# Reading x transposed from DRAM for ten token tiles, with a feature map and a weight sum moved between engines

## The chip, the cores and the metric

The kernel runs on one core of one Trainium2 chip. The metric is device time in microseconds (us) of one execution of the whole program. Engines are named as the profile names them: PE (TensorE matmul), PEld (its weight load), DVE (VectorE), ACT (ScalarE), POOL (GpSimd) and SP (SyncE, which here issues the DMAs).

## The reference

One block is computed over S = 2048 tokens of D = 576 features, in float32:

```
xn  = layernorm(x)                                # per token, eps 1e-5, no scale or shift
q, k, v = split(xn @ wqkv)                        # 32 heads of 18 features
phi(t) = where(t > 0, t + 1, exp(t)) + 1e-6
kv  = sum over tokens of phi(k)^T v               # per head, 18 x 18
z   = sum over tokens of phi(k)                   # per head
s   = ((phi(q) @ kv) / (phi(q) . z + 1e-6)) @ wo
g   = silu(gelu(xn @ w1 + b1) @ w2 + b2)          # hidden size F = 4608
out = x + s * g
```

## The kernel before, in words

Every matrix product is made of two-part operands: a tensor is rounded to a "hi" part (an ACT copy that casts to fp32r) and the remainder is its "lo" part (a DVE subtraction). A product then is hi*hi + hi*lo + lo*hi on PE. Two large products (w1 and w2) are cut into 2 x 2 blocks and done with seven block products instead of eight, so they need sums and differences of blocks (on POOL), whose hi and lo parts are formed as well.

The work has three phases, written one after the other. Within phases 1 and 2 every engine follows the program's order (`in_order()`), and in phase 3 DVE, ACT, POOL and PE do. So what an engine executes next is fixed by the code; an instruction that waits holds up all that is queued behind it on its engine.

**Phase 1** is a loop over 16 token tiles of 128 tokens (`for t in range(NT)`, L464). One turn is called a slot here. In slot t PE does: `project` into `pk` (k and the first part of v, 28 matmuls), `transpose_x(t + 1)` (five 128 x 128 transposes of the normalised x, L212), `state` of the tile before (its sum of phi(k)^T v into `ps_kva`, `ps_kvb`, L293), and `project` into `pv` (the rest of v, 14 matmuls). Around that, DVE takes the statistics of tile t + 2 (`layernorm`), ACT normalises it (`normalize_x`, L201), and ACT and DVE split the transposed x into `xh` and `xl`. The feature map `phi` is an ACT exponential (L262), a DVE minimum with 1 (L264), and a DVE maximum against the projection (L266). POOL adds phi(k) to `zacc` (L523), the source of z. PSUM has three two-bank buffers (`bank2`), handed out in turn to `pk`, `pt`, `pv`, and two one-bank buffers (`bank1`).

Beside this, phase 1 prepares weights for phase 3. For each of nine chunks of w2, `w2_sum` forms three block differences (`T_OPS = (5, 6, 4)`) on POOL, `w2_hi` and `w2_lo` split them on ACT and DVE, and `w2_store` writes them to DRAM; `we_sums`, `we_hi`, `we_lo` do the same for five groups of the last rows of w1. Four stores of x blocks to `x_dram` (`X_STORES`) are issued in slots 11 to 14, and `make_mask` runs on POOL in slot 7.

**Between phases 1 and 2** PE does `query(0)` (the q projection of tile 0), the last `state`, two matmuls into `zb_ps` that spread z over all partitions (L548), and `query(1)`. ACT copies `zb_ps` to `zb` (L549). Then ACT and DVE do `phi` for q of tiles 0 and 1 (`phi_query(0)`, `phi_query(1)`), and `fold_wo` multiplies the masked kv with wo: six blocks of two matmul results each (L604), written to `bank1` buffers in turn and copied out by ACT (L611, L613) or DVE (L609), before `query(2)`.

**Phase 2** is a loop over the tiles: `query(i)`, `transpose_p(i - 2)`, `attend(i - 4)` on PE, `phi_query(i)` and the denominators beside it.

**Phase 3** takes 18 steps, nine chunks of the hidden size for each half of the tokens. A step has 28 places (`NS = 28`). Places 0 to 13 are two `Up` units of seven block products each, in the order `UP = (1, 6, 7, 5, 2, 3, 4)`; places 14 to 27 are the `product` calls with w2, in the order `ORDER = (1, 2, 7, 4, 5, 3, 6)`. After each place, `at_step` emits what the plan put there: `base + place`. In the first half (steps 0 to 8) the plan also holds the preparation of w1 and w2: `sum7` on POOL at place 2, the `hi` and `lo` of w2 operands 1, 2 and 7 at places 3 to 6 (`PW2`), and loads of the operands 4, 5 and 6 that phase 1 stored. In the second half all operands are loaded. Within an `Up`, product 5 goes to the PSUM bank `E`, DVE adds it to `B` (L1047), and product 3, two products later, accumulates onto `E`, so it must wait for that addition. `HOps.S` forms the sums of the gelu outputs on POOL (L1111, L1114, L1117, L1120), and their `lo` parts are at L707, as are those of w2.

```
PW2 = {1: 3, 2: 4, 7: 5, 3: 20}
W2_SUMS_NEXT = {4: 21, 5: 23, 6: 27}
W2_SUMS_FIRST = {4: 4, 5: 6, 6: 10}
W2_LOADS = {0: (0, 1), 1: (2,), 3: (3,), 4: (4,), 6: (5,), 8: (6,), 9: (7,), 12: (8,)}
```

Of the kernel before, what the change touches and what calls it, by code (L numbers as in the profile page):

```python
# [15 lines left out]
P = 128  # L16
# [8 lines left out]
KT = 5  # L25
# [14 lines left out]


@with_exitstack
def linear_attention_gated_ffn(ctx, tc, x, wqkv, wo, w1, w1e, b1, w2, b2, out):
# [94 lines left out]
    ones = t1.tile([P, P], F32, name="ones", bufs=1)  # L138
    nc.gpsimd.memset(ones, 1.0)
# [4 lines left out]
    def make_mask():  # L144

        nc.gpsimd.memset(mf, 1.0)
# [26 lines left out]
    def layernorm(t):  # L173
# [3 lines left out]
        mv = t1.tile([P, 4], F32, tag="mv", name=f"mv{t}")  # L177
        nc.vector.bn_aggr(mv[:, 0:2], st)
        nc.vector.tensor_scalar_add(mv[:, 2:3], mv[:, 1:2], 1e-5)
        nc.gpsimd.tensor_tensor(mv[:, 3:4], mv[:, 2:3], nhalf, op=ALU.pow)  # L180
        stats[t] = mv
        if t == 0:
            xn[t] = t1.tile([P, 640], F32, tag="xn", name=f"xn{t}")
            for dst, src in norm_parts(t):
                nc.vector.tensor_scalar(dst, src, mv[:, 0:1], mv[:, 3:4], op0=SUB, op1=MUL)

    def offset(t):

        mv = stats[t]
        nc.vector.scalar_tensor_tensor(  # L190
            mv[:, 2:3], mv[:, 0:1], -1.0, mv[:, 3:4], op0=MUL, op1=MUL
        )
# [4 lines left out]
    def normalize_x(t):  # L197
        mv = stats.pop(t)
        xn[t] = t1.tile([P, 640], F32, tag="xn", name=f"xn{t}")
        for dst, src in norm_parts(t):  # L200
            nc.scalar.activation(dst, src, AF.Identity, scale=mv[:, 3:4], bias=mv[:, 2:3])  # L201
# [29 lines left out]

    PARTS = [p + str(k) for k in range(KT) for p in ("hh", "hl", "lh") if (p, k) != ("lh", KT - 1)]
# [25 lines left out]
    VB = 512 - HD  # L258

    def phi(pool, ps, name, between=lambda: None):  # L260
        e = pool.tile([P, D], F32, tag="e", name=f"e{name}")
        nc.scalar.activation(as2(e), ps[:, :, :HD], AF.Exp)  # L262
# [3 lines left out]
        nc.vector.scalar_tensor_tensor(  # L266
            as2(r), ps[:, :, :HD], 1.000001, as2(e), op0=ADD, op1=ALU.max
        )
        return r, e
# [17 lines left out]
    zacc = t1.tile([P, D], F32, name="zacc", bufs=1)  # L287
    ps_kv = []

    def state(t, k_t, v_t):  # L290
        for i, (g, n) in enumerate(GROUPS):
            dst = ps_kv[0][:n, g : g + n] if i < 4 else ps_kv[1][:n, :n]
            nc.tensor.matmul(  # L293
                dst, v_t[:, g : g + n], k_t[:, g : g + n],
                start=(t == 0 and i in (0, 4)), stop=(t == NT - 1), skip_group_check=True,
            )
# [3 lines left out]
    T_OPS = (5, 6, 4)  # L300
    w2raw, w2op = {}, {}

    def w2_load(c):
        if c == 2:
            t = x_hi(2, "w2r2")
        elif c == 5:
            t = x_hi(3, "w2r5")
        else:
            t = w2p.tile([P, CF * D], F32R, tag="w2r", name=f"w2r{c}")
        t = t.bitcast(F32) if c not in (2, 5) else t.bitcast(F32).rearrange("p a b -> p (a b)")  # L310
        nc.sync.dma_start(t[:, : CF * D], w2[c])
        w2raw[c] = t[:, : CF * D].rearrange("p (a r n d) -> p a r n d", a=2, r=2, n=2)

    def w2_block(c, i):

        B = lambda r, n: w2raw[c][:, :, r, n, :]
        return {
            5: (B(0, 0), B(0, 1), B(0, 0)),
            6: (B(1, 1), B(1, 1), B(0, 0)), 4: (B(1, 0), B(1, 0), B(1, 1)),
        }[i]  # L320

    def w2_sum(j):
        c, i = j // 3, T_OPS[j % 3]
        dst, a, b = w2_block(c, i)
        nc.gpsimd.tensor_tensor(dst, a, b, op=SUB)  # L325

    def w2_hi(j):
# [5 lines left out]
        nc.scalar.copy(w2op[j][:, 0], w2_block(j // 3, T_OPS[j % 3])[0])  # L333

    def w2_lo(j):
        c, i = j // 3, T_OPS[j % 3]
        t = w2op[j]
        nc.vector.tensor_tensor(t[:, 1], w2_block(c, i)[0], t[:, 0].bitcast(F32), op=SUB)

    def w2_store(j):  # L340
        c, i = j // 3, T_OPS[j % 3]
# [21 lines left out]
    def we_op(q, v):  # L363
        return we["h", q % 2][:, v * WB * P : (v + 1) * WB * P]
# [8 lines left out]
    def we_store(q):  # L373
        src = we["h", q % 2][:, : 2 * WB * P].bitcast(F32)
# [3 lines left out]
    W2_LOADS = {0: (0, 1), 1: (2,), 3: (3,), 4: (4,), 6: (5,), 8: (6,), 9: (7,), 12: (8,)}  # L378
    W2_SUMS = {}
    for j in range(3 * NC):  # L380
        W2_SUMS.setdefault(1 + j // 2, []).append(j)
# [52 lines left out]
    def query(t):  # L434
# [24 lines left out]
    X_STORES = {  # L459
        11: lambda: (0, xh[0][:, :4]), 12: lambda: (4, xl[0]),  # L460
        13: lambda: (10, xh[1][:, 2:4]), 14: lambda: (14, xl[1][:, 2:]),
    }
    raw_q = {}
    for t in range(NT):  # L464
        for n in (3, 4) if t == 0 else (t + 4,):
# [4 lines left out]
        if 0 < t < NT - 2:  # L470
            layernorm(t + 2)
        pk = bank2(f"pk{t}")
        v_t = t1.tile([P, D], F32, tag="v", name=f"v{t}")
        if t == 0:
# [8 lines left out]
            project(t, wv_h, wv_l, pv, FIRST_V[0], end=False)  # L483
        else:
            project(t, wkv_h, wkv_l, pk, cols=(slice(0, HD), slice(HD, D + VB)))
            k_t, _ = phi(t1, pk, f"k{t}", lambda: nc.scalar.copy(v_t[:, :VB], pk[:, 1, HD:]))
        if t + 1 < NT:
            if t + 1 in (8, 12):
                x_block((t + 1) // 4)
            transpose_x(t + 1)  # L490
        if t == 0:
            project(t, wv_h, wv_l, pv, FIRST_V[1], begin=False)
        for j in W2_SUMS.get(t - 1, ()):
            w2_hi(j)
        for j in W2_SUMS.get(t - 1, ()):
            w2_lo(j)
        if 2 <= t < 2 + WG:
            we_hi(t - 2), we_lo(t - 2)
        if t == 0:
            layernorm(2)  # L500
        if t + 2 < NT:
            offset(t + 2)
        if t == 0:
            k_t, _ = phi(t1, pk, f"k{t}")
# [4 lines left out]
        if t == 0:  # L509
            nc.scalar.copy(as2(v_t), pv[:, :, :HD])  # L510
        else:
            pv = bank2(f"pv{t}")
            project(t, wkv_h, wkv_l, pv, cols=(slice(D + VB, 2 * D),))
            nc.scalar.copy(v_t[:, VB:], pv[:, 0, : D - VB])
        if t + 2 < NT:
            normalize_x(t + 2)
        if t == 0:
            nc.gpsimd.memset(zacc, 0.0)
        for j in W2_SUMS.get(t, ()):
            w2_sum(j)  # L520
        if 1 <= t < 1 + WG:
            we_sums(t - 1)
        nc.gpsimd.tensor_tensor(zacc, zacc, k_t, op=ADD)  # L523
# [6 lines left out]
        if 2 <= t < 2 + WG:  # L530
            we_store(t - 2)
            if t < WG:
                we_load(t)
        for c in W2_LOADS.get(t, ()):
            w2_load(c)
        if t == KT + 2:
# [3 lines left out]
        if t in X_STORES:  # L540
            at, src = X_STORES[t]()
            nc.sync.dma_start(x_dram[:, at : at + src.shape[1]], src.bitcast(F32))
# [3 lines left out]
    zb_ps = bank2("zb_ps")  # L546
    for h in range(2):
        nc.tensor.matmul(zb_ps[:, h, :HD], ones, zacc[:, h * HD : (h + 1) * HD], start=True, stop=True)  # L548
    nc.scalar.copy(as2(zb), zb_ps[:, :, :HD])  # L549
# [3 lines left out]
    nc.vector.copy_predicated(kvz[:ln, D:], mask[:ln, 8:ln], ps_kv[1][:ln, 8:ln])  # L553
    ph1.close()
# [7 lines left out]
    def load_w2_raw(n):  # L562
        raw = w2rp.tile([P, CF // 2, 2, 2, HD], F32, tag="w2raw", name=f"w2raw{n}")
        nc.sync.dma_start(raw.rearrange("p a b n d -> p (a b n d)"), w2[n % NC])
# [392 lines left out]

    for i in range(1, NT + 4):
        if i < NT:
            query(i)  # L960
        if i == 1:
# [100 lines left out]
    class W2:  # L1062
# [5 lines left out]
        def load_raw(self):  # L1068
            self.raw = raw = load_w2_raw(self.n) if self.n else w2_raw0[0]
            self.B = lambda r, n: raw[:, :, r, n, :]  # L1070
# [4 lines left out]

        def plain(self, f):
            self.src["p", f] = self.raw[:, f // 2, f % 2]
# [301 lines left out]
    for step in range(n_chunks):  # L1379
# [139 lines left out]
```

## Time and profile before

| what | value |
| --- | --- |
| time, median of 3 runs | 1100.94 us (1100.39 to 1101.23) |
| the profiled execution's own time | 1101.18 us |
| its span, first to last instruction | 1099.5 us |
| PE busy | 1092.2 us (99%) |
| DVE busy | 809.3 us (74%) |
| ACT busy | 456.2 us (41%) |
| POOL busy | 452.0 us (41%) |
| granted TensorE clock | 1.000 |

The span lies inside the execution's own time. Busy time is the time in which an engine has an instruction under way. A timeline row gives the start, the time for all its instructions together, the engine, the source line, the operation, the tile written and those read, the shape, and in brackets how long the engine sat idle before and what ended that. A row of the chain that ended last gives the start, the time it holds, and its engine and line. Matmuls overlap at their ends, so a matmul row's time is a little more than its share of the chain.

### The profile page before, as it was taken

Reading aid. Unit: us, or ns where it says so; the run is one execution under the profiler, and the core shown is the slowest. Engines: PE = TensorE matmul, PEld = TensorE weight load, DVE = VectorE, ACT = ScalarE, POOL = GpSimd, SP = SyncE. Lnnn points to the kernel's source line nnn. Section 1 sums busy time; section 2 is a strip of 40 time slices with the busy share of each in tenths; the row PEclk is TensorE's granted clock in tenths of the full one; section 3 lists DMA queues with packets and bytes.
Section 4 is the critical chain, followed back from the end, with each engine's and each line's share of the span. In section 5 each row is a group of like instructions: output and inputs, shape, how many; then the busy total and the mean of one; then the engine's idle time right before and its main releaser. Section 6 shows DMA issues by size and latency. Waiting matters only on the chain.

```text
span 1099.5 us, 18157 instructions
## 1 busy us (share of the span) xinstructions
PE 1092.2 (99%) x6762; PEld 1006.8 (92%) x6762; DVE 809.3 (74%) x1162; ACT 456.2 (41%) x787; POOL 452.0 (41%) x392
## 2 busy tenths in 40 slices
PE   9999999999999999999999999999999999999998
PEld 8999989999998998989989899899898998989988
DVE  7786558989687887978878878667485574764866
ACT  5555444343644354454443544524234242242342
POOL 4786434333354452453534633324234143242340
PEclk9999999999999999999999999999999999999999
DMA  8697852575978659576595689978776676766452
GB/s 331 226 369 278 288 193 64 171 234 181 318 265 317 214 186 338 187 274 250 185 347 176 242 288 391 395 259 283 225 229 223 204 231 219 242 216 216 136 183 87
DMA packets 84655, 265.57 MB, mean 242 GB/s; under 512 B 9942, under 2 KB 20694, under 8 KB 80728
## 3 DMA queue, kind: packets, MB, share of 16 engines
q1 hardware_dynamic: 84568, 264.42, 68.7%
q8 instruction: 53, 0.87, 0.3%
q14 instruction: 34, 0.28, 0.1%
HBM read 166.69 MB, written 95.75 MB: 239 GB/s over the span
## 4 chain that ended last, share of the span: by engine, by line
PE 98%; DMA 0%; DVE 0%; issue 0%; ACT 0%; SPq 0%; DVEq 0%; ACTq 0%
PE pm L1154 35%; PE a L1021 10%; PE e L1021 10%; PE zy L1021 10%; PE pk L250 7%; PE ps_s L680 5%; PE pq L250 5%; PE b L1021 5%; PE pv L250 3%; PE pd L1270 2%; PE ps_kva L293 1%; PE ptp L662 1%; PE pt L212 1%; PE ps_kw L604 1%; DMA w<-wqkv 0%
## 5 line engine op out<-in xcount | busy, mean ns | idle before, releaser
L1160 DVE TENSOR_TENSOR macc<-pm,macc 128x576 f32<-128x576 f32 x218 | 163.6, 750 | 54.6 <-PE pm L1154 53.8
L704 ACT CAST h_h<-g 128x512 fp32r<-128x512 f32 x204 | 120.8, 620 | 132.5 <-PE pm L1154 131.4
L707 DVE TENSOR_TENSOR h_l<-g,h_h 128x512 fp32r<-128x512 f32 x204 | 164.9, 815 | 0.0
L1120 POOL TENSOR_TENSOR mid<-g 128x512 f32<-128x512 f32 x34 | 43.9, 1290 | 125.9 <-ACT g L1029 125.9
L1114 POOL TENSOR_TENSOR g<-g 128x512 f32<-128x512 f32 x34 | 54.8, 1613 | 56.9 <-DVE h_l L707 55.6
L1029 ACT ACTIVATE g<-b,b1c 128x512 f32<-128x512 f32 x36 | 24.8, 688 | 115.8 <-DVE b L1047 115.8
L1038 ACT COPY mid<-a 128x512 f32<-128x512 f32 x36 | 21.1, 587 | 117.2 <-PE a L1021 117.2
L750 POOL TENSOR_TENSOR w1raw<-w1raw 128x256 f32<-128x256 f32 x18 | 16.9, 939 | 122.0 <-DVE wa L766 122.0
L1041 DVE TENSOR_TENSOR mid<-b,mid 128x512 f32<-128x512 f32 x36 | 24.7, 686 | 44.6 <-PE b L1021 43.1
L1242 POOL TENSOR_TENSOR fin1l<-fin1h,fin1l 128x288 f32<-128x288 f32 x8 | 6.5, 810 | 121.6 <-DMA fin1l<-s_dram 107.2
L1117 POOL TENSOR_TENSOR g<-g 128x512 f32<-128x512 f32 x34 | 55.2, 1624 | 2.7
L1021 PE MATMUL a<-h0r,wa 128*128 128x512 f32 x144 | 50.4, 391 | 0.0
L1021 PE MATMUL a<-xh,wa 128*128 128x512 f32 x144 | 50.4, 390 | 0.0
L707 DVE TENSOR_TENSOR h_l<-mid,h_h 128x512 fp32r<-128x512 f32 x34 | 48.9, 1438 | 1.2
L1111 POOL TENSOR_TENSOR g<-g 128x512 f32<-128x512 f32 x34 | 46.8, 1376 | 2.7
L1047 DVE TENSOR_TENSOR b<-e,mid 128x512 f32<-128x512 f32 x36 | 25.2, 699 | 30.3 <-PE e L1021 30.3
L645 POOL TENSOR_TENSOR pbuf<-phiq,den 128x576 f32<-128x576 f32 x16 | 20.8, 1298 | 63.1 <-DVE den L644 44.3
L1044 DVE TENSOR_TENSOR mid<-zy,mid 128x512 f32<-128x512 f32 x36 | 24.9, 691 | 24.6 <-PE zy L1021 24.6
L325 POOL TENSOR_TENSOR w2r<-w2r 128x576 f32<-128x576 f32 x27 | 39.6, 1472 | 7.9 <-DMA w2r<-w 7.2
L250 PE MATMUL pk<-wkv_l,xh 128*128 128x288 f32 (+1 forms) x160 | 41.9, 343 | 0.1
L250 PE MATMUL pk<-wkv_h,xh 128*128 128x288 f32 (+1 forms) x160 | 41.3, 341 | 0.5 <-ACT wkv_h L280 0.5
L264 DVE TENSOR_SCALAR ek<-ek 128x576 f32<-128x576 f32 x16 | 12.8, 798 | 38.0 <-ACT ek L262 38.0
(826 smaller groups left out, 3563.7 us busy)
## 6 DMA issues: line engine op xcount, KB each, us to landing
we<-we_dram SPq DMA_DIRECT2D x36, 448.0 KB
op<-w2o SPq DMA_DIRECT2D x27, 576.0 KB
w2raw<-w SPq DMA_DIRECT2D x10, 1152.0 KB
w2r<-w SPq DMA_DIRECT2D x9, 1152.0 KB
w1raw<-w SPq DMA_DIRECT2D x18, 512.0 KB
op_a<-wa SPq DMA_DIRECT2D x18, 512.0 KB
op_c<-wc SPq DMA_DIRECT2D x18, 512.0 KB
op_d<-wd SPq DMA_DIRECT2D x18, 512.0 KB
```

The source lines that it names most:

```text
L250: nc.tensor.matmul(ps[:, h, : ws.stop - ws.start], st, w[:, k, ws], start=(begin and i == 0), stop=(end and i == len(seq) - 1), skip_group ...
L325: nc.gpsimd.tensor_tensor(dst, a, b, op=SUB)
L680: nc.tensor.matmul(ps[:, h, :HD], st[:, k, :], w[:, k, h * HD : (h + 1) * HD], start=(i == 0), stop=(i == len(seq) - 1),)
L704: nc.scalar.copy(pair[0], src)
L707: eng.tensor_tensor(pair[1], src, pair[0].bitcast(F32), op=SUB)
L1021: nc.tensor.matmul(ps, st, mv, start=first and n == 0, stop=n == len(seq) - 1, skip_group_check=True,)
L1111: tt(src[5, pr], A(1, 0), A(1, 1), op=ADD)
L1114: tt(src[6, pr], src[5, pr], A(0, 0), op=SUB)
L1117: tt(src[3, pr], A(0, 1), src[6, pr], op=SUB)
L1120: tt(src[7, pr], A(0, 0), A(1, 0), op=SUB)
L1154: nc.tensor.matmul(ps[:, q, :HD], hs[p][st][:, cs], m[:, p, :], start=(n == 0 and i not in CHAIN), stop=(n == 5), skip_group_check=True,)
L1160: nc.vector.tensor_tensor(dst, src, dst, op=ADD)
```

## The change

The change has these parts.

1. For tiles 6 to 15 (`NTR = 6`), x is read from a second input `xT` that holds x transposed, so `transpose_x` is left out for them. The statistics of tile t are taken in slot t - 5, stored to DRAM (`store_stats`), loaded back spread over all partitions in slot t - 3 (`load_stats`), subtracted on POOL in slot t - 2 (`center`) and multiplied on DVE in slot t - 1 (`scale`), where ACT and DVE also split the result (`set_x_hi`, `set_x_lo`). Tiles 0 to 5 go the old way.
2. In `phi`, exp with a minimum becomes three ACT instructions: relu of the negative, exp of the negative of that, and an addition of 1e-6. DVE keeps only the maximum. This holds for k in phase 1 and for q in phase 2.
3. z is no longer summed in `zacc`. The v tiles hold a column of ones in each group, so `state` also yields the sums of phi(k) in row 126. After the last `state` ACT copies them out (`sums_k`); `query(1)` goes ahead of the two `zb_ps` matmuls. v is copied in groups (`copy_v`), and `pk` takes 126 columns of v instead of 224 (`VB = G`), `pv` the other 450.
4. Operand 4 of w2 is no longer made in phase 1. In phase 3 it is made from w2 itself by two POOL subtractions (`sum4`) at place 5 of steps 0 to 8, with `hi` at place 8 and `lo` with a store at place 9; `PW2` has 2 ahead of 1. The loads of operand 4 in the first half fall away. w2 lies in DRAM in another order of blocks, so that phase 1 loads three of the four.
5. The timing of phase 1's side work changes: `w2_sum` at slots 2, 4, 6, 8, 10 to 14, `we_sums` at slots 1, 3, 5, 7, 9; `make_mask` in slot 15; the four x stores in turns 3 to 6 of phase 2.

```
+NTR = 6
...
+    def load_xt(t):
+        if t == NTR:
+            xn[t - 1] = xt_tile(f"xn{t - 1}")
+        raw = xt_tile(f"xt{t}")
+        xts[t] = raw.rearrange("p (k c) -> p k c", k=KT)
+        nc.sync.dma_start(raw, xT[t])
+    def store_stats(t):
+        st_dram[t] = dram.tile([P, 2], F32, name=f"st_dram{t}")
+        nc.sync.dma_start(st_dram[t], stats.pop(t)[:, :2])
+    def load_stats(t):
+        bcs[t] = t1.tile([P, P, 2], F32, tag="bc", name=f"bc{t}", bufs=3)
...
+    def center(t):
+        nc.gpsimd.tensor_tensor(xts[t], xts[t], of_tokens(t, 0), op=SUB)
+    def scale(t):
+        nc.vector.tensor_tensor(xts[t], xts[t], of_tokens(t, 1), op=MUL)
+    def set_x_hi(t):
+        xt, h, _, cs = x_tile(t)
+        nc.scalar.copy(h[:, :, cs], xt)
+    def set_x_lo(t):
+        xt, h, l, cs = x_tile(t)
+        nc.vector.tensor_tensor(l[:, :, cs], xt[:, :4], h[:, :4, cs].bitcast(F32), op=SUB)
+        nc.vector.tensor_tensor(h[64:, 4, cs], xt[64:, 4], h[64:, 4, cs].bitcast(F32), op=SUB)
...
-        nc.scalar.activation(as2(e), ps[:, :, :HD], AF.Exp)
+        nc.scalar.activation(as2(e), ps[:, :, :HD], AF.Relu, scale=-1.0)
         between()
-        nc.vector.tensor_scalar(e, e, 1.0, 1e-6, op0=ALU.min, op1=ADD)
+        nc.scalar.activation(e, e, AF.Exp, scale=-1.0)
+        nc.scalar.activation(e, e, AF.Identity, bias=tiny[:, 0:1])
...
+    def ones_columns():
+        for v in v_bufs:
+            nc.gpsimd.memset(v, 0.0)
+            nc.gpsimd.memset(v[:, :, G : G + 1], 1.0)
+    def copy_v(v, g, ps):
+        n = ps.shape[1] // G
+        nc.scalar.copy(v[:, g : g + n, :G], ps[:, : n * G].rearrange("p (g c) -> p g c", c=G))
+        if n * G < ps.shape[1]:
+            nc.scalar.copy(v[:, g + n, : ps.shape[1] - n * G], ps[:, n * G :])
...
-    T_OPS = (5, 6, 4)
+    T_OPS = (5, 6)
...
+        if NTR <= t + 3 < NT:
+            load_xt(t + 3)
+            load_stats(t + 3)
+        if NTR <= t + 5 < NT:
+            statistics(t + 5)
+            store_stats(t + 5)
+        if NTR <= t + 2 < NT:
+            center(t + 2)
+        if NTR <= t + 1 < NT:
+            scale(t + 1)
...
+            if t == 0:
+                ones_columns()
+                k_t, _ = phi(t1, pk, f"k{t}")
...
-        nc.gpsimd.tensor_tensor(zacc, zacc, k_t, op=ADD)
...
     query(0)
     state(*pend)
...
+    nc.scalar.copy(sums_k[96 : G + 1, : 4 * G], ps_kv[0][96 : G + 1, : 4 * G])
+    nc.scalar.copy(sums_k[96 : G + 1, 4 * G :], ps_kv[1][96 : G + 1, :ln])
+    query(1)
+    zb_ps = bank2("zb_ps")
+    for h in range(2):
+        nc.tensor.matmul(
+            zb_ps[:, h, :HD], last_row[: G + 1], sums_k[: G + 1, h * HD : (h + 1) * HD],
+            start=True, stop=True,
+        )
+    nc.scalar.copy(as2(zb), zb_ps[:, :, :HD])
...
+        def sum4(self, k):
+            self.src[4] = t = self.src[2]
+            nc.gpsimd.tensor_tensor(t, t, self.src[(7, 1)[k]], op=SUB)
...
-    PW2 = {1: 3, 2: 4, 7: 5, 3: 20}
-    W2_SUMS_NEXT = {4: 21, 5: 23, 6: 27}
-    W2_SUMS_FIRST = {4: 4, 5: 6, 6: 10}
+    PW2 = {2: 3, 1: 4, 7: 5, 4: 8, 3: 20}
+    W2_SUMS_NEXT = {5: 23, 6: 27}
+    W2_SUMS_FIRST = {5: 6, 6: 10}
...
             add(base + 2, w2t[step].sum7)
+            for k in range(2):
+                add(base + 5, w2t[step].sum4, k)
```

More of the change, by code (lines that the diff above doesn't have):

```diff
@@ L39, with linear_attention_gated_ffn @@
 NWARM = 20
+NTR = 6
 @with_exitstack
[L43 removed]
+def linear_attention_gated_ffn(ctx, tc, x, xT, wqkv, wo, w1, w1e, b1, w2, b2, out):
     nc = tc.nc
@@ L482, in linear_attention_gated_ffn @@
             pv = bank2(f"pv{t}")
-            project(t, wv_h, wv_l, pv, FIRST_V[0], end=False)
+            v_cols = slice(0, 3 * G), slice(3 * G, D)
+            project(t, wv_h, wv_l, pv, FIRST_V[0], cols=v_cols, end=False)
         else:
             project(t, wkv_h, wkv_l, pk, cols=(slice(0, HD), slice(HD, D + VB)))
[L486 to L489, printed above, removed]
+        values = lambda: copy_v(v_t, 0, pk[:, 1, HD : HD + VB])
+        if t + 1 < NTR:
+            if t:
+                k_t, _ = phi(t1, pk, f"k{t}", values)
             transpose_x(t + 1)
[L491 to L504, printed above, removed]
+            if t == 0:
+                project(t, wv_h, wv_l, pv, FIRST_V[1], cols=v_cols, begin=False)
+            for j in sums2:
+                w2_hi(j)
+            for j in sums2:
+                w2_lo(j)
+            if t - 1 in WE_SUMS:
+                we_hi(WE_SUMS[t - 1]), we_lo(WE_SUMS[t - 1])
+            if t == 0:
+                layernorm(2)
+            if t + 2 < NTR:
+                offset(t + 2)
+            if t == 0:
+                ones_columns()
+                k_t, _ = phi(t1, pk, f"k{t}")
+        else:
+            if not last:
+                set_x_hi(t + 1), set_x_lo(t + 1)
+            for j in sums2:
+                w2_hi(j)
+            for j in sums2:
+                w2_lo(j)
+            if t - 1 in WE_SUMS:
+                we_hi(WE_SUMS[t - 1]), we_lo(WE_SUMS[t - 1])
+            k_t, _ = phi(t1, pk, f"k{t}", values)
         if pend is not None:
@@ L509, in linear_attention_gated_ffn @@
         if t == 0:
-            nc.scalar.copy(as2(v_t), pv[:, :, :HD])
+            for i, cs in enumerate(v_cols):
+                copy_v(v_t, 3 * i, pv[:, i, : cs.stop - cs.start])
         else:
@@ L545, in linear_attention_gated_ffn @@
     state(*pend)
[L546 to L549, printed above, removed]
     ln = GROUPS[-1][1]
```

166 lines of the change are left out of this document (94 added, 72 removed).

## The prediction

> **What bounds the kernel now.** I read the page first: its span, the busy times and the engines of the chain that ended last.
>
> ```profile
> span 1099.5 us, 18157 instructions
> PE 1092.2 (99%) x6762; PEld 1006.8 (92%) x6762; DVE 809.3 (74%) x1162; ACT 456.2 (41%) x787; POOL 452.0 (41%) x392
> PE 98%; DMA 0%; DVE 0%; issue 0%; ACT 0%; SPq 0%; DVEq 0%; ACTq 0%
> ```
>
> PE is busy for 99% of the span and is 98% of the chain. So two things count: how much work PE loses, and whether PE now has to wait anywhere. Relief for DVE, ACT, POOL or the DMA queue is worth nothing by itself. The second view is the chain in order of time, for the length of a slot of phase 1 with and without transposes, and for a turn of phase 2.
>
> ```profile
> 52.94 5.09 PE pk L250 x28
> 58.02 0.55 PE pt L212 x5
> 61.84 1.22 PE pk L250 x7
> 142.16 5.09 PE pk L250 x28
> 150.52 3.70 PE pq L250 x28
> ...
> 203.47 0.55 PE ptp L662 x5
> 207.72 3.70 PE pq L250 x28
> ```
>
> A slot with transposes lasts 61.84 - 52.94 = 8.90 us; the last slot, which has none, 150.52 - 142.16 = 8.36 us. Five transposes are worth 0.54 us, as their own row says.
>
> **Part 1, the transposes.** Slots 5 to 14 lose them: 10 x 0.54 = 5.4 us less PE work. That is all the change takes from PE. The other matmuls keep their columns: `pk` has 98 fewer per step and `pv` 98 more. This is a gain only if x arrives without them. Each slot now needs on SP a load of xT, a load of the spread statistics and a small store; on POOL `center`; on DVE `scale`. The window of one early slot of before shows the engines at their fullest (busy of PE, PEld, DVE, ACT, POOL, then clock, DMA share and GB/s):
>
> ```profile
> 52.94:61.84 8.90, 8.90 (x59) 8.28 (x59) 7.65 (x15) 5.12 (x9) 8.37 (x8) 1.00 1.01 388
> ```
>
> POOL at 8.37 and the DMA engines at 1.01 did not hold PE up here. The new slots are lighter: w2 sums and w1 sums no longer fall in one slot, `zacc` is gone, w2 is loaded by three quarters, a third of its stores and the x stores are elsewhere, against `center` and about 0.5 MB. Statistics have two slots, some 16 us, from the store to their load, and each later step has a slot; SP's `store_stats` waits for POOL's power, with `w2_store` and the next x behind it, whose users come a slot later. I cost all this at nothing; should the cover fail, it eats the 0.54 us of a slot and more (a rival below). `make_mask` moved into the last slot has POOL to itself, and the x stores meet a phase 2 without urgent loads.
>
> **Part 2, the start.** In slot 0 `ones_columns` puts two pairs of memsets on POOL behind a power that waits for DVE, and ACT's copy of v must wait for them, with the normalisation of tile 2 queued behind it.
>
> ```profile
> 17.32 0.64 ACT L510 COPY v<-pv 128x576 f32<-128x576 f32 x1 [0.22 <-PE pv L250]
> 19.18 0.55 POOL L180 TENSOR_TENSOR mv<-mv,nhalf 128x1 f32<-128x1 f32 x1 [5.39 <-DVE mv L179]
> 19.67 0.58 POOL L518 MEMSET zacc<- 128x576 f32 x1
> 19.95 1.20 ACT L201 ACTIVATE xn<-x,mv 128x576 f32<-128x576 f32 x2 [1.99 <-DVE mv L190]
> 22.21 0.71 PE L212 MATMUL pt<-ident,xn 128*128 128x128 f32 x5
> ```
>
> The power ends at 19.73. A memset 640 wide takes 0.58 x 640/576 = 0.64, the short one some 0.1, so ACT copies v from 20.5. Three copies instead of one of 0.64 take an estimated 0.9, and 1.20 of normalisation ends at 22.6, not 21.15. PE reaches the transposes at about 21.6: 28 matmuls of 288 columns take 3.70, or 0.132 each, so one of 512 takes (5.09 - 14 x 0.132) / 14 = 0.23, one of 414 about 0.19, and `pk` ends 0.6 earlier. Four of the five transposes need only the first part of the tile, so they spread out and end near 22.7 instead of 22.2: 0.5 us lost, between 0 (memsets early) and 1.1 (all five wait for the end).
>
> **Part 3, phi in three steps, and the turn to phase 2.**
>
> ```profile
> 154.06 1.04 PE L293 MATMUL ps_kva<-phik,v 128*126 128x126 f32 x8
> 155.07 1.18 PE L548 MATMUL zb_ps<-zacc,ones 128*128 128x288 f32 x4
> 156.29 0.64 ACT L549 COPY zb<-zb_ps 128x576 f32<-128x576 f32 x1 [4.13 <-PE zb_ps L548]
> 156.82 0.66 ACT L262 ACTIVATE eq<-pq 128x576 f32<-128x576 f32 x1
> 158.01 0.76 DVE L266 SCALAR_TENSOR_TENSOR phiq<-pq,eq 128x576 f32<-128x576 f32 x1
> 159.80 7.52 PE L604 MATMUL ps_kw<-wo,kvz 126*126 126x288 f32 x24
> 160.06 0.65 ACT L262 ACTIVATE eq<-pq 128x576 f32<-128x576 f32 x1 [2.58 <-PE pq L250]
> 160.61 0.77 ACT L611 COPY kw<-ps_kw 126x288 f32<-126x288 f32 x2
> 166.94 0.65 PE L250 MATMUL pq<-wq_h,xh 128*128 128x288 f32 x2
> ```
>
> `fold_wo` has two one-bank buffers, so PE goes on only as ACT copies them out; from the first copy to `query(2)` it took 166.94 - 160.61 = 6.33. ACT came to that copy just behind the exponential of tile 1. In the new order the zb matmuls follow `query(1)`: 155.07 + 3.70 = 158.77, and the copy of zb starts 1.22 later, as before, at 159.99. Behind it on ACT, though tile 0's q has long been there, stand six instructions in place of two. Independent ones start 0.53 to 0.55 apart (156.29 to 156.82, 160.06 to 160.61), dependent ones 0.66 and an estimated 0.05 for the signal. So 160.52, 161.23, 161.94 for tile 0, 162.49, 163.20, 163.91 for tile 1, and the first copy of kw at 164.46 instead of 160.61: 3.8 us, all of it on PE. Bounds: 3.2 (all six 0.55 apart) and 4.2 (all 0.71).
>
> Elsewhere the longer `phi` is covered. In phase 2 `pq`'s buffer must be free when the next `pq` starts, 207.72 - 203.47 = 4.25 after its end; three times 0.65 and 0.76 with signals are 2.9. Slots 1 to 4 have a similar margin; without it each slot would lose the shortfall. I take 0.
>
> **Part 4, operand 4 of w2 in phase 3.** This is where a new wait arises. The timeline of DVE at places 4 to 10 of one step of the first half:
>
> ```profile
> 430.17 0.75 DVE L707 TENSOR_TENSOR w__4886<-w2raw,w__4886 128x576 fp32r<-128x576 f32 x1
> 431.44 0.68 DVE L766 TENSOR_TENSOR wd<-w1raw,wd 128x512 fp32r<-128x512 f32 x1
> 432.04 0.75 DVE L707 TENSOR_TENSOR w__4905<-w2raw,w__4905 128x576 fp32r<-128x576 f32 x1
> 432.71 0.69 DVE L1058 TENSOR_TENSOR zy<-zy,mid 128x512 f32<-128x512 f32 x1
> 434.66 1.38 DVE L766 TENSOR_TENSOR wa<-w1raw,wa 128x512 fp32r<-128x512 f32 x1 [0.60 <-ACT wa L761]
> 435.97 0.68 DVE L1041 TENSOR_TENSOR mid<-b,mid 128x512 f32<-128x512 f32 x1
> 437.12 0.69 DVE L1044 TENSOR_TENSOR mid<-zy,mid 128x512 f32<-128x512 f32 x1 [0.47 <-PE zy L1021]
> 438.71 0.70 DVE L1047 TENSOR_TENSOR b<-e,mid 128x512 f32<-128x512 f32 x1 [0.89 <-PE e L1021]
> ```
>
> and of ACT, POOL and PE in the same step:
>
> ```profile
> 433.44 0.69 ACT L1029 ACTIVATE g<-zy,b1c 128x512 f32<-128x512 f32 x1 [0.51 <-DVE zy L1058]
> 427.65 1.43 POOL L1074 TENSOR_TENSOR w2raw<-w2raw 128x576 f32<-128x576 f32 x1
> 434.20 1.30 POOL L1120 TENSOR_TENSOR mid<-g 128x512 f32<-128x512 f32 x1 [5.12 <-ACT g L1029]
> 435.58 1.62 POOL L1111 TENSOR_TENSOR g<-g 128x512 f32<-128x512 f32 x1
> 440.10 1.52 PE L1021 MATMUL e<-s,wc 128*128 128x512 f32 x6
> ```
>
> DVE's `wa` took 1.38 where `wd`, of the same shape, took 0.68: POOL's L1120 ran until 435.50, and `wa` ended 0.54 after that. POOL's next took 1.62 and not 1.30, waiting in turn. L1041, with an input in PSUM, took 0.68 in the middle of it. So a DVE subtraction from SBUF and a POOL one exclude each other.
>
> The first `sum4` can start when the lo of operand 2 is done, at 430.98, and by L1074's 1.43 ends at 432.41; `wd` ends 0.54 later at 432.95; the second `sum4` then at 434.38; the 576-wide lo after it at 434.98. L1058 starts 2.2 late, at 434.93. Gelu, POOL's L1120, ACT's `wa`, DVE's `wa` and L1041 follow each other and are 2.2 late too: L1041 at 438.15. L1044's 0.47 of idle time is used up: 438.76. Then comes lo of operand 4, 0.67 from start to start, into L1047's idle 0.89, and L1047 starts at 440.04 and ends at 440.74. PE's product 3 onto `E` started at 440.10. PE waits 0.7 us in each of nine steps: 6.3 us. Bounds per step: 0 (no exclusion; 0.67 fits in 0.89) and 2.2 (no idle time absorbs any). I take 0.7, since each delay in it is read from a row of the same step, and 0.3 to 1.2 as its own spread. Nothing pays for it on PE: the loads of operand 4 that fall away were not waited for.
>
> By start to start, L1120 holds POOL for 435.58 - 434.20 = 1.38, against its span of 1.30. The Trainium skill ("Perfetto Trace Analysis", GPSIMD Engine Instruction) says that GpSimd spans should not be trusted and that spacing should be used. With 0.08 more for each of the two sums the wait would be 0.86 a step, and the whole 1.4 us more.
>
> **The sum**, against the profiled execution's 1101.18 us (its span and 1.7 around it): -5.4 + 0.5 + 3.8 + 6.3 = +5.2. The median is 0.24 below that execution, so I forecast 1100.94 + 5.2 = 1106.1 us.
>
> **Rivals.** (a) The first half of phase 3 takes the new work without a wait: POOL finds its two sums a place where DVE does not queue behind them. For it speaks that POOL is idle for 5.12 before L1120; against it that DVE has its own SBUF subtractions in just that stretch. It decides where L1047 starts under 0.7 late. Then -5.4 + 0.5 + 3.8 = -1.1: 1099.8, and with the lower bounds of the start and the turn -2.2: 1098.7. Not slower.
>
> (b) PE comes out of the fold slower than it went in. It would stand from about 160.4 to 164.9.
>
> ```profile
> 1.56 4.53 PE L286 MATMUL warm<-ident 128*128 128x128 f32 x20 [1.56 <-POOL ident masks.py:199]
> ```
>
> After idling at the start, 20 transposes took 4.53, or 0.23 each, against 0.55/5 = 0.11 in a slot; all idle time of PE in before is 1099.5 - 1092.2 = 7.3 us. At half rate ten fold results, some 0.4 of matmul each, add 0.2 to 0.4 each: +2.5, 1108.6. The Trainium skill ("TensorE: Matmul & The Clock Gate", Part 1) states that a window of about 3.4 us without work halves the clock until a busy window has passed; the row of the start agrees, and no trace yet shows such a gap inside the kernel.
>
> (c) The change does not bring what it says: DVE and POOL, excluding each other in `center`, `scale`, `set_x_lo` and `w2_lo`, make the slots as long as before. Against it speaks the early slot above, fuller and without a wait. The 5.4 are gone: 1111.5.
>
> **How the numbers follow.** Forecast 0.50, (a) 0.23, (b) 0.16, (c) 0.11. A change of 0.2%, 2.2 us, is about the least that a measurement of this kernel can tell from none. Faster by more than that is the lower half of (a): 0.12. Within it are the rest of (a) and the forecast's lightest corner: 0.13. Slower: 0.75. The forecast's own range, with 0.3 to 1.2 a step, is 1102 to 1111; the range down to 1098.5 and up to 1113 takes in (a), (b) and most of (c).
>
> **What would show it.** Slots 5 to 14 at 8.36; `pt` of tile 2 with a wait for ACT; `query(2)` 3.8 later against the last `state`; in each of steps 0 to 8 an idle PE before `e` with L1047's counterpart as releaser, L1058's 2 us later in its step, and steps of 45.4 instead of 44.7. I am wrong if those steps keep their length, or if the fold starts copying on time.

## The result, and the profile after

The changed kernel takes 1117.09 us (median; 1116.67 to 1118.45), the kernel before on the same chip 1100.83 (1100.39 to 1101.23). The ratio is 1.015 (95% interval 1.0132 to 1.0168): slower by 16.3 us, where 5.2 were forecast. The profiled execution lasted 1116.67 us. Its page, span, busy times and the engines of the chain that ended last:

```profile
span 1114.9 us, 18103 instructions
PE 1095.0 (98%) x6712; PEld 1009.5 (91%) x6712; DVE 825.0 (74%) x1130; ACT 491.0 (44%) x850; POOL 467.5 (42%) x401
PE 77%; DVE 10%; DMA 5%; ACT 3%; issue 3%; POOL 1%; SPq 1%; ACTq 0%; DVEq 0%
```

PE was 98% of the chain and is 77%. The span grew by 15.4, PE's busy time by 2.8: nearly all the loss is PE waiting. The chain in order of time (start, us, what) gives the lengths of the stages: two early slots, two slots without transposes, and a turn of phase 2.

```profile
26.43 4.47 PE pk L315 x28
35.42 4.49 PE pk L315 x28
...
61.92 4.49 PE pk L315 x28
66.42 0.88 PE ps_kva L375 x8
67.30 0.18 PE ps_kvb L375 x2
67.47 2.92 PE pv L315 x14
70.39 1.72 PE pk L315 x11
...
201.10 3.73 PE pq L315 x28
209.10 3.73 PE pq L315 x28
```

Slots with transposes last 9.0 us (8.91 in before), those without 8.45 (8.36 in before's last slot), turns of phase 2 8.01 (7.95). The table divides the span at the first matmul of a stage in PE's timeline, which lies 0.1 to 0.4 ahead of the chain's times:

| stage | before | after | difference | forecast |
|---|---|---|---|---|
| start, to `pk` of slot 2 | 26.03 | 26.26 | +0.2 | +0.5 |
| slots 2 to 15 | 124.33 | 119.99 | -4.3 | -5.4 |
| turn, `query(0)` to `query(2)` | 16.58 | 21.89 | +5.3 | +3.8 |
| phase 2, `query(2)` to step 0 | 120.13 | 120.89 | +0.8 | 0 |
| steps 0 to 8 | 401.96 | 415.40 | +13.4 | +6.3 |
| step 9 to the end | 410.47 | 410.47 | 0 | 0 |

**The turn.** The timeline of ACT and PE (start, duration, engine, line; in brackets the idle time before it and what ended it), and the window of the rest of the fold with the granted clock in the seventh place behind the length:

```profile
155.99 0.64 ACT L649 COPY zb<-zb_ps 128x576 f32<-128x576 f32 x1 [3.42 <-PE zb_ps L645]
156.53 0.66 ACT L328 ACTIVATE eq<-pq 128x576 f32<-128x576 f32 x1
157.21 0.68 ACT L330 ACTIVATE eq<-eq 128x576 f32<-128x576 f32 x1
157.93 0.78 ACT L331 ACTIVATE eq<-eq,tiny 128x576 f32<-128x576 f32 x1
...
160.67 0.68 ACT L707 COPY kw<-ps_kw 126x288 f32<-126x288 f32 x2
161.10 7.42 PE L700 MATMUL ps_kw<-wo,kvz 126*126 126x288 f32 x20 [4.17 <-ACT kw L707]
162.00:168.52 6.52, 6.52 (x20) 3.26 (x19) 2.25 (x7) 2.27 (x6) 2.52 (x2) 0.74 0.29 89
```

Six ACT instructions stand ahead of the first copy of `kw`, PE waits 4.17 us for it, and comes out of the wait at a mean granted clock of 0.74 instead of 1.00.

**One step of the first half.** DVE, POOL and PE in step 3 (427.56 to 473.76):

```profile
437.62 3.27 POOL L1181 TENSOR_TENSOR w2raw<-w2raw 128x576 f32<-128x576 f32 x2 [2.00 <-DVE w__4855 L803]
437.99 1.61 DVE L862 TENSOR_TENSOR wd<-w1raw,wd 128x512 fp32r<-128x512 f32 x1
439.53 1.98 DVE L803 TENSOR_TENSOR w__4874<-w2raw,w__4874 128x576 fp32r<-128x576 f32 x1
441.43 0.69 DVE L1160 TENSOR_TENSOR zy<-zy,mid 128x512 f32<-128x512 f32 x1
446.74 0.69 DVE L1149 TENSOR_TENSOR b<-e,mid 128x512 f32<-128x512 f32 x1
447.49 1.65 PE L1123 MATMUL e<-s,wc 128*128 128x512 f32 x6 [0.68 <-DVE b L1149]
...
450.79 0.43 PE L1262 MATMUL pm<-w__4874,h_h 128*128 128x288 f32 x2
...
454.77 0.62 ACT L800 CAST h_h<-mid 128x512 fp32r<-128x512 f32 x1 [1.41 <-POOL mid L1228]
455.42 1.24 DVE L803 TENSOR_TENSOR h_l<-mid,h_h 128x512 fp32r<-128x512 f32 x1 [0.42 <-ACT h_h L800]
460.00 0.74 DVE L1268 TENSOR_TENSOR macc<-pm,macc 128x576 f32<-128x576 f32 x1
460.89 0.51 PE L1262 MATMUL pm<-w__4942,h_h 128*128 128x288 f32 x2 [0.29 <-DVE macc L1268]
```

PE in the same step of before (421.01 to 465.68), at the first product with w2 and at product 4:

```profile
443.27 0.42 PE L1154 MATMUL pm<-w__4886,h_h 128*128 128x288 f32 x2
...
452.85 0.46 PE L1154 MATMUL pm<-w__4706,h_h 128*128 128x288 f32 x2
```

While POOL forms operand 4, DVE's `wd` takes 1.61 (0.68 before) and the lo of operand 1 takes 1.98 (0.75 before). L1160, counterpart of L1058, starts 13.87 into the step, 2.2 later than in before. L1149 is late for product 3 on `E`, and PE waits: it starts that product 19.93 into the step, 0.84 later than in before (440.10 less 421.01); that is the 0.7 of the forecast. But a second wait follows in the product half: from its first product to product 4 it takes 10.10 us, 9.58 in before. The late gelu makes POOL's L1228 late, with it ACT's cast and DVE's L803 at 455.42; the `macc` additions are queued behind that, and product 4, which accumulates onto product 7's buffer (`CHAIN`), must wait until DVE has read it.

### The profile page after: what moved, and what is told of

It is laid out like the page before. It is cut to its first block, busy times and chain, and to the rows that moved or that the text cites. A ratio compares the mean times of both kernels' runs of the same rounds, so it can differ in the third digit from the quotient of the medians.

```text
span 1114.9 us, 18103 instructions
## 1 busy us (share of the span) xinstructions
PE 1095.0 (98%) x6712; PEld 1009.5 (91%) x6712; DVE 825.0 (74%) x1130; ACT 491.0 (44%) x850; POOL 467.5 (42%) x401
## 4 chain that ended last, share of the span: by engine, by line
PE 77%; DVE 10%; DMA 5%; ACT 3%; issue 3%; POOL 1%; SPq 1%; ACTq 0%; DVEq 0%
PE pm L1262 29%; PE a L1123 7%; PE e L1123 6%; PE zy L1123 6%; PE pk L315 6%; PE pq L315 5%; PE pv L315 4%; PE ps_s L776 4%; PE b L1123 4%; DVE h_l L803 3%; PE pd L1378 2%; DMA op_a<-wa 2%; PE ps_kva L375 1%; DVE wd L862 1%; DVE macc L1268 1%
## 5 line engine op out<-in xcount | busy, mean ns | idle before, releaser
L803 DVE TENSOR_TENSOR h_l<-g,h_h 128x512 fp32r<-128x512 f32 x204 | 165.0, 815 | 0.0
L1228 POOL TENSOR_TENSOR mid<-g 128x512 f32<-128x512 f32 x34 | 43.9, 1291 | 97.3 <-ACT g L1131 97.3
L1143 DVE TENSOR_TENSOR mid<-b,mid 128x512 f32<-128x512 f32 x36 | 24.7, 686 | 43.7 <-PE b L1123 43.0
L803 DVE TENSOR_TENSOR h_l<-mid,h_h 128x512 fp32r<-128x512 f32 x34 | 48.8, 1436 | 4.9 <-ACT h_h L800 3.7
L1149 DVE TENSOR_TENSOR b<-e,mid 128x512 f32<-128x512 f32 x36 | 25.1, 697 | 22.5 <-PE e L1123 22.5
L1131 ACT ACTIVATE g<-zy,b1c 128x512 f32<-128x512 f32 x36 | 24.8, 688 | 38.4 <-DVE zy L1160 38.4
L1156 DVE TENSOR_TENSOR e<-e,mid 128x512 f32<-128x512 f32 x36 | 24.8, 690 | 19.8 <-PE e L1123 19.8
L1131 ACT ACTIVATE g<-e,b1c 128x512 f32<-128x512 f32 x36 | 24.8, 690 | 33.0 <-DVE e L1156 33.0
L315 PE MATMUL pk<-wkv_h,xh 128*128 128x288 f32 (+1 forms) x160 | 38.2, 321 | 0.9 <-DVE xh L245 0.9
```

The source lines that it names most:

```text
L315: nc.tensor.matmul(ps[:, h, : ws.stop - ws.start], st, w[:, k, ws], start=(begin and i == 0), stop=(end and i == len(seq) - 1), skip_group ...
L803: eng.tensor_tensor(pair[1], src, pair[0].bitcast(F32), op=SUB)
L1131: nc.scalar.activation(g, ps, AF.Gelu_apprx_tanh, bias=b1c[:, f : f + 1])
L1228: tt(src[7, pr], A(0, 0), A(1, 0), op=SUB)
```

## Experiments

Each kernel is compared with the kernel before on the same chip.

**1. Phase 3 without the two POOL subtractions.**

```
 self.src[4] = t = self.src[2]
-nc.gpsimd.tensor_tensor(t, t, self.src[(7, 1)[k]], op=SUB)
```

> The changed kernel without the two POOL subtractions that form operand 4 of w2 in phase 3 (sum4 is left out, so operand 4 is plain block (1,0)); its cast, its lo part, its store and everything else stay. Theory: POOL's two subtractions keep DVE's subtractions from SBUF out, and all of the 1.5 us by which steps 0 to 8 are longer follows from that; the lo of operand 4 itself (0.67) fits into the 0.89 that DVE waited there. Then steps of 44.7 to 44.9 and a time of 1103.7 to 1105.5 us. Rival: the added work of ACT and DVE and the added store make the steps longer, whatever POOL does: steps stay at 46.0 or more and the time at 1114 or more. Between: the sums cost the 0.7 that the prediction worked out and the rest of operand 4 the other 0.8: steps of 45.4, 1110 us.

Measured: 1107.05 us (ratio 1.0053, 1.0038 to 1.0068). DVE in step 3 of its trace, which begins at 424.00 and ends at 468.71:

```profile
434.43 0.68 DVE L862 TENSOR_TENSOR wd<-w1raw,wd 128x512 fp32r<-128x512 f32 x1
435.70 0.69 DVE L1160 TENSOR_TENSOR zy<-zy,mid 128x512 f32<-128x512 f32 x1
440.72 0.75 DVE L803 TENSOR_TENSOR w__4934<-w2raw,w__4934 128x576 fp32r<-128x576 f32 x1
441.70 0.70 DVE L1149 TENSOR_TENSOR b<-e,mid 128x512 f32<-128x512 f32 x1 [0.23 <-PE e L1123]
```

`wd` is back at 0.68, and steps 0 to 8 take 44.67 to 44.72. The lo of operand 4 is still there, and DVE has time for it: of the 0.89 that DVE waited there in before it uses 0.67 and leaves 0.23, as the prediction had it. Steps 0 to 8 together take 402.40, so 13.0 of their 13.4 us come from the two POOL subtractions; the cast, the lo part and the store cost at most the other 0.4, which was not divided further. The median lies 1.6 above the expected range. The trace's span of 1103.2 is within it, although its slot 12 lost 0.9 (experiment 7); what the other executions lost is not shown.

**2. The same subtractions at another place.** At place 0 POOL works on w2 before it works on w1. In this order sum4 overwrites block (1,0) before operand 2 is formed from it, so operand 2 has other values; no instruction is left out or added.

```
+add(base, w2t[step].sum7)
+for k in range(2): add(base, w2t[step].sum4, k)
 plan_w1(add, w1t[2 * step + 1], base, **P1)
-add(base + 2, w2t[step].sum7)
-for k in range(2): add(base + 5, w2t[step].sum4, k)
```

> The changed kernel with sum7 and both sum4 at place 0 of the step, ahead of the w1 sums, instead of places 2 and 5: POOL is idle for 13.7 us before the w1 sums, while DVE mostly waits for PE. Nothing is left out. Theory (POOL and DVE exclude each other, and only the place counts): steps near 44.8 and 1104 to 1106.5 us; some is lost where the sums now meet DVE's casts of w1 at places 26 to 0. Rival (the work of operand 4 costs it, wherever it is): 1116 to 1118 us. A third outcome: the block of w2 lands too late for place 0, the w1 sums wait behind it, and the step is longer than in the changed kernel: over 1118.

Measured: 1105.66 us (1.0043, 1.0028 to 1.0058), steps of 44.69 to 44.77. POOL and DVE in step 3, from 424.88:

```profile
426.31 3.60 POOL L1181 TENSOR_TENSOR w2raw<-w2raw 128x576 f32<-128x576 f32 x2
...
427.83 0.79 DVE L862 TENSOR_TENSOR wa<-w1raw,wa 128x512 fp32r<-128x512 f32 x1 [1.05 <-ACT wa L857]
428.55 0.68 DVE L1143 TENSOR_TENSOR mid<-b,mid 128x512 f32<-128x512 f32 x1
435.31 0.68 DVE L862 TENSOR_TENSOR wd<-w1raw,wd 128x512 fp32r<-128x512 f32 x1
```

The same POOL work, spread over 3.60 us, is nearly free here: the nine steps take 402.48, within 0.1 of experiment 1. DVE waited for ACT and PE in 1.7 of these microseconds, and L1143, which it did in them, has an input in PSUM. So the cost lay in the place. The Trainium skill ("SBUF — State Buffer", Who interferes with whom) states that a DVE instruction with two SBUF inputs contends with a GpSimd instruction that reads SBUF, and that the second of them is blocked until the first ends. The 1.61 and 1.98 beside L1181, and 0.68 for L1143, whose `b` lies in PSUM, agree.

**3. The turn in another order.** `zb`'s copy goes behind the feature map of tile 0, that of tile 1 behind the fold.

```
 phi_query(0)
-phi_query(1)
+nc.scalar.copy(as2(zb), zb_ps[:, :, :HD])
 normalize(0)
 fold_wo()
+phi_query(1)
```

> The changed kernel with the copy of zb behind the feature map of q tile 0, and the feature map of tile 1 behind the fold of wo. Theory (the six steps of the feature map ahead of the first copy of the fold set the turn, and the 4.17 us in which PE stands idle halve its clock for a while after): the first copy of the fold follows the copy of zb, at about 156.5 instead of 160.7, the fold takes 6.3 instead of 7.4, and query of tile 2 starts some 5 us earlier: 1112 us, 1111 to 1114. Rival: the chain behind z (POOL's product with zb, the denominators of tile 0) sets the turn, and nothing is gained, or the feature map of tile 1, now late, takes back what was gained when its PSUM buffer is needed: 1116 to 1119.

Measured: 1114.19 us (1.0122, 1.0105 to 1.0139), 0.2 above the expected range.

```profile
156.22 7.46 PE L699 MATMUL ps_kw<-wo,kvz 126*126 126x288 f32 x24
172.94 0.74 PE L757 MATMUL ptp<-ident,pbuf 128*128 128x128 f32 x5 [1.25 <-DVE phiq L333]
```

The fold runs through without the wait, and `query(0)` to `query(2)` takes 16.62, not 21.9: the turn's 5.3 come from the ACT queue ahead of the fold, with the lower clock behind it (experiment 4). Both theories are half right, though: the late feature map of tile 1 holds a PSUM buffer, and the next two turns lose 1.9.

**4. The clock by itself.** PE is kept busy in the idle stretch by transposes that nobody uses; the wait for ACT stays.

```
+if (i, n, h) == (1, G, 0):
+    for _ in range(30): nc.tensor.transpose(zb_ps[:, 0, :P], ident, ident)
```

> The changed kernel with 30 useless transposes of the identity on PE, into the PSUM buffer of zb after its copy, in the stretch in which PE waits 4.17 us for the first copy of the fold. Theory (the idle stretch lowers the clock, a granted 0.74 over the next 6.5 us): the transposes take 30 x 0.11 = 3.3 of the 4.17, the idle time falls under 1 us, the fold takes 6.3 to 6.5 instead of 7.42 at a granted clock of 1.0, and the whole is 1.0 to 1.3 us shorter: 1115.9. Rival (the fold is paced by ACT's copies and not by PE's clock): the fold stays at 7.4 whatever the clock, and the time at 1117.1, or longer by what the transposes overrun.

Measured: 1117.26 us (1.015, 1.0135 to 1.0165). PE's timeline, and the window of the fold's later part:

```profile
160.12 3.44 PE L702 MATMUL zb_ps<-ident 128*128 128x128 f32 x30
164.47 6.27 PE L703 MATMUL ps_kw<-wo,kvz 126*126 126x288 f32 x20 [0.90 <-ACT kw L710]
164.47:170.74 6.27, 6.26 (x22) 2.99 (x23) 3.15 (x8) 2.63 (x7) 2.52 (x2) 1.00 0.19 60
```

With 0.90 of idle time the clock stays at 1.00, and the same 20 matmuls take 6.27, not 7.42: the idle stretch cost 1.15 us beyond itself. In two other traces with the 4.17 they took 7.51 (experiment 1) and 8.27 (experiment 2), so the price is 1.2 to 2.0. The Trainium skill ("TensorE: Matmul & The Clock Gate", Part 1) states that about 3.4 us without work halves the clock, in windows that run freely; the 4.17 and the varying price agree. The gain is shown by the trace alone (`query(0)` to `query(2)` takes 20.75 and not 21.89). The median did not show it: in this profiled execution slots 11 and 12 lost 3.6 us (experiment 7), and a gain of 1.2 lies within the spread of the runs.

**5. The feature map of before.**

```
-nc.scalar.activation(as2(e), ps[:, :, :HD], AF.Relu, scale=-1.0)
+nc.scalar.activation(as2(e), ps[:, :, :HD], AF.Exp)
 between()
-nc.scalar.activation(e, e, AF.Exp, scale=-1.0)
-nc.scalar.activation(e, e, AF.Identity, bias=tiny[:, 0:1])
+nc.vector.tensor_scalar(e, e, 1.0, 1e-6, op0=ALU.min, op1=ADD)
```

> The changed kernel with the feature map of before: an exponential on ACT and a minimum on DVE instead of three ACT steps; everything else as changed. Theory: at the turn the first copy of the fold comes after four ACT instructions fewer (2 x 1.4), some 2.8 us earlier, PE's idle time falls from 4.17 to about 1.4 and the clock stays, which is worth another 1.2: query of tile 2 starts 4 us earlier; in phase 1 DVE has 0.4 a slot more to do and may be late where slot 12 already loses up to 1.1: 1112.5 to 1114. If theory 2 of the run with the longer constant tile holds, turns of phase 2 go back to 7.95 and it is 0.8 less. Rival (z's new way over ps_kva, sums_k and zb_ps behind query 1 sets the turn, not the feature map): 1116 to 1117.5.

Measured: 1113.62 us (1.0117, 1.01 to 1.0134).

```profile
156.17 1.20 ACT L328 ACTIVATE eq<-pq 128x576 f32<-128x576 f32 x2
157.24 0.72 ACT L706 COPY kw<-ps_kw 126x288 f32<-126x288 f32 x2
157.72 3.23 PE L699 MATMUL ps_kw<-wo,kvz 126*126 126x288 f32 x10 [1.15 <-ACT kw L706]
```

PE waits 1.15 and not 4.17, and `query(0)` to `query(2)` takes 18.5, 3.4 less: that is what the longer feature map (part 2 of the change) costs at the turn, lower clock included. The remaining 1.9 against before are put down, by elimination, to the new order around `zb`, whose matmuls and copy now follow `query(1)`; no run puts back that order alone. Turns of phase 2 stay at 8.01, so the longer feature map is not what made them longer.

**6. The address of the tiles.** Nothing but the length of the new constant tile differs.

```
-tiny = cst.tile([P, 1], F32, name="tiny")
+tiny = cst.tile([P, 16], F32, name="tiny")
```

> The changed kernel with its new constant tile (one value per partition, 4 bytes, padded to 32) made 64 bytes long, so that the tiles allocated behind it on the same side (the q weights, the transposed p and others) lie 64 bytes lower than in the kernel before and not 32. Nothing else changes. Question: a turn of phase 2 takes 8.01 us in every trace of the changed code and 7.95 before, with the same matmuls and a granted clock of 1.00. Theory 1 (the address of an operand sets the spacing of matmuls of 288 columns): turns of 7.95, 0.8 us less in all, 1116.3. Theory 2 (the longer feature map or other work of ACT and DVE beside PE sets it): 8.01 and 1117.1.

Measured: 1117.19 us (1.0149, 1.0134 to 1.0164). The chain in phase 2:

```profile
206.52 3.64 PE ps_s L776 x28
210.16 3.65 PE pq L315 x28
214.35 3.72 PE ps_s L776 x28
```

The same matmuls took 3.73 in every turn of the changed kernel; here, from 206 on, those of every second turn take 3.64 or 3.65. Turns are 7.91 (7.95 in before, 8.01 in the changed kernel), and phase 2 takes 119.97 (120.13 and 120.89). So the tiles' places changed PE's speed by 1%, at a granted clock of 1.00 each time. The 0.8 us that the change lost in phase 2 fit the same cause, but no run puts the tiles back where before had them, so that part is not shown. Why the places count, and why in every second turn only, stays open. The gain did not reach the median; in the trace slot 12 lost 1.4.

**7. Both moves, done so that they pay.** In phase 3 operand 2 is split first and the sums follow at place 0; at the turn the steps of tile 1's feature map stand between copies of the fold, where ACT waited for PE. Then the same with the longer constant tile.

```
+add(base + 27, w2t[step + 1].hi, 2)          # in the step before
+add(base, w2t[step].lo, 2); add(base, w2t[step].sum7)
+for k in range(2): add(base, w2t[step].sum4, k)
...
+            if i >= 2:
+                next(steps)                   # in fold_wo: one step of phi of tile 1
```

> The changed kernel with two moves, nothing left out. In phase 3 operand 2's cast goes to place 27 of the step before and its lo part to place 0, and sum7 and both sum4 follow there, ahead of the w1 sums. At the turn the copy of zb stands behind the feature map of q tile 0, and the three ACT steps of tile 1's feature map stand between the copies of the fold. Theory: 13.4 - 0.4 from the steps (44.7) and 5.3 + 1.9 x 0 from the turn without the 1.9 us that the late feature map of tile 1 cost: 1117.1 - 11.6 - 5 = 1100.5, 1099 to 1102.5. Rival: the sums, now behind operand 2's lo part, end later and the w1 sums behind them hold up the first w1 operands: steps of 45.2 or more, 1105 or more.

> The same two moves with the constant tile 64 bytes long. Theory 1 of the run with the longer constant tile: 0.8 us less than the two moves alone, 1099.7; theory 2: the same time as the two moves alone.

Measured: 1101.01 us (1.0005, 0.9995 to 1.0014) and 1100.17 us (0.9994, 0.9985 to 1.0003). Steps take 44.72, the turn 16.6; turns of phase 2 take 8.01 with the short constant and 7.91 with the long one. But step 0 takes 46.44 in both. PE's wait in it, and the one of ACT ahead of it:

```profile
293.03 0.41 ACT L871 CAST w<-w1t 128x256 fp32r<-128x256 f32 x1 [5.21 <-POOL w1t L863]
...
296.59 0.50 PE L1137 MATMUL a<-xh,wa 128*128 128x512 f32 x1 [0.96 <-ACT g L1145]
```

In step 0 operand 2 is cast only inside the step, so the sums and with them the w1 sums are late. Two further versions, with the longer constant tile, put that work before the step loop, and the second also moves most of the w1 sums of phase 1 one or two slots forward:

```
-WE_SUMS = {2 * q + 1: q for q in range(WG)}
+WE_SUMS = {1: 0, 2: 1, 3: 2, 5: 3, 7: 4}
```

> The two moves and the 64-byte constant tile, and for step 0 of phase 3 operand 2's cast, its lo part, sum7 and both sum4 before the first step, since step 0 took 46.44 us with the two moves where every later one took 44.72. Theory: step 0 at 44.7, 1.7 us less than the kernel with both moves and the longer tile: 1098.5. Rival: the same work stands in the way at the end of phase 2 instead, and the 1.7 stays: 1100.2.

> As the kernel before it in this list, and the sums of the last rows of w1 in slots 1, 2, 3, 5 and 7 of phase 1 instead of 1, 3, 5, 7 and 9, so that the last of their stores, whose tile is x block 3's hi part, leaves two slots earlier. Theory: the up to 1.4 us that slot 12 lost in five of nine traces came from ACT's first cast of block 3, which waited for that store; without it the median falls by about 0.5 and the spread narrows: 1098. Rival: the early slots now are too full (POOL, DMA), and a slot of 2 to 4 is longer: 1098.5 to 1101.

Measured: 1098.44 us (0.9978, 0.9969 to 0.9987) and 1097.99 us (0.9975, 0.9965 to 0.9984): both are faster than the kernel before, by 0.2%. Step 0 takes 44.9. What the second one is about, in the trace of experiment 6 and, in the last row, in the second version's own:

```profile
102.92 0.32 SPq L447 DMA_DIRECT2D we_dram<-w1h  x1
111.06 0.73 ACT L289 CAST xh<-xt 128x640 fp32r<-128x640 f32 x1 [6.49 <-DMA we_dram<-w1h]
118.04 1.15 PE L375 MATMUL ps_kva<-phik,vb 128*127 128x126 f32 x8 [0.75 <-DVE phik L333]
...
104.58 0.74 ACT L289 CAST xh<-xt 128x640 fp32r<-128x640 f32 x1
```

The last store of w1's sums was issued at 102.92 and still held the tile of x block 3 at 111.06; ACT's first cast into that tile and all behind it were late, and PE waited in slots 11 or 12. In all ten traces with the old slots this cast waits for that store. In five of them it starts at 110.86 or later and PE loses 0.9 to 3.6 us; in the other five it starts between 107.67 and 110.40 and PE loses nothing. With the sums moved it starts at 104.58 and waits for no store. So the wait and its cause are shown; why the store lands later in some executions is not, and four of the five come from one chip. What removing the wait is worth in the median is not: the two medians differ by 0.45, but their intervals overlap. The page of the last version:

```profile
span 1096.5 us, 18080 instructions
PE 1088.9 (99%) x6712; PEld 1008.5 (92%) x6712; DVE 803.3 (73%) x1130; ACT 491.6 (45%) x850; POOL 469.5 (43%) x401
PE 97%; DVE 1%; DMA 1%; issue 0%; ACT 0%; SPq 0%; POOL 0%; DVEq 0%
```

With as many instructions on each of these engines as in the changed kernel, PE is 97% of the chain again.

**8. Addresses in phase 3.**

```
+pad3.tile([P, 8], F32, name="pad3")           # ahead of phase 3's tiles on the right side
```

> As the kernel before it, with 32 bytes left free ahead of phase 3's tiles on the right side, so that the operands of the products with w2 lie 32 bytes lower. If what the 64-byte constant did to the turns of phase 2 (8.01 to 7.91) holds for the products as well, steps change from 44.66 by up to 0.5 us either way; if phase 3 doesn't feel the address, they stay within 0.02.

Measured: 1097.87 us (0.9972, 0.996 to 0.9984), steps of 44.64 to 44.72: phase 3 feels the address by 0.04 a step at most.

## Why the prediction was right and where it was wrong

**The direction and the cause were right**: slower, by the forecast's own mechanism, with POOL's sum4 and DVE's subtractions excluding each other, L1160 about 2.2 us late, product 3 on `E` 0.84 late against 0.7, and 0.23 left ahead of L1149 without it. The time lies 4 us above the wider of the two ranges, at 1113, because four terms were off in the same direction: part 4 by 7.1 us, the turn by 1.5, part 1 by 1.1 and phase 2 by 0.8.

**Part 4, 6.3 forecast, 13.4 measured.** The failed step is the end of the sum: it followed the lateness to product 3 and stopped there. In step 3 the `Up` half takes 23.23 against 22.26, so 0.97 where 0.7 was forecast: product 3 starts 0.84 late, and its first six matmuls take 1.65 and not 1.52. With the spacing of POOL's instructions, which the Trainium skill ("Perfetto Trace Analysis", GPSIMD Engine Instruction) asks for, the prediction had 0.86. The product half takes 22.97 against 22.41: another 0.56, at product 4, which the sum did not have. L1149 starts 1.48 later in its step than in before. Over the late gelu DVE's L803 at 455.42 is 1.49 late, and from there DVE has no idle time until 469 (in before from 447.38 until 461), so that the `macc` addition at 460.00, which product 4 waits for, is still 1.50 late. PE paid that lateness in two parts, at product 3 and at product 4. The prediction's spread of 0.3 to 1.2 a step left out 1.5. Its upper bound of 2.2 held it, but did not go into the range.

**The turn, 3.8 forecast, 5.3 measured.** The first copy of the fold came at 10.69 after the start of the last `state`, against 6.55 in before: 4.1, where 3.85 were forecast; the instruction with the constant tile took 0.78 and not 0.66, twice. The Trainium skill ("ScalarE: Activation LUTs", What ACT_TABLE_LOAD costs) gives about 93 ns for such an operand; 0.78 beside the 0.68 of the exponential agrees. The rest is rival (b), taken as an alternative with 0.16 where it was a further term: the forecast itself had PE stand for over 4 us, and the three folds behind 4.17 us of it (experiment 4) were all slower. It cost 1.2 to 2.0; 2.5 was given.

**Part 1, 5.4 forecast, 4.3 measured.** The slots without transposes take 8.45, not 8.36, and early slots 9.0, not 8.91. The step that failed is "the other matmuls keep their columns": the moved columns and the wider v tile in `state` cost about 0.09 a slot (`pk` 0.60 less, `pv` 0.65 more by the chain, `ps_kvb` 0.05 more). That x would come without a wait held in the profiled execution. In traces of other versions slots 11 and 12 lost 0.9 to 3.6 (experiment 7). The prediction only said that the cover might fail; it looked at the stores of phase 1 for their number, not for the tile that one of them holds.

**Phase 2, 0 forecast, 0.8 measured**: the longer feature map is covered, as said; the places of tiles, to which the 0.8 may be due, are not a thing that the prediction considered.

The start cost 0.2, within its 0 to 1.1. Rivals (a) and (c) did not come: no step kept its length, and slots did become shorter.

## What to carry to other kernels

When a delayed engine is followed to the first instruction that makes PE wait, the sum is not finished: follow its queue until it has idle time again, and add each place where PE depends on it. POOL work on SBUF is priced by what DVE does in the same microseconds, so first look for a stretch in which DVE waits or reads PSUM; here the same two subtractions cost 13.0 us at place 5 and about 0.1 at place 0. A wait of PE that is worked out to be as long as the 4.17 us here should be given a clock term along with it; after 0.90 (experiment 4) the clock stayed at 1.00.

## What the runs showed of the hardware that was not expected

Moving the tiles of one side of SBUF by 32 bytes changed the time of 28 unchanged matmuls of 288 columns from 3.73 to 3.65 in every second turn of phase 2, at a granted clock of 1.00, while 32 bytes in phase 3 changed next to nothing. After 4.17 us of idle time the same 20 matmuls took 7.42, 7.51 or 8.27 us in different executions, and 6.27 when PE had been kept busy.
